# Element-wise work of an attention and two-MLP kernel moved off GpSimd, and the second MLP's weights converted earlier

## The chip, the cores and the metric

One core of one Trainium2 chip runs the kernel. The metric is device time in microseconds (us) of one execution. Before the change three runs took 1559.98, 1563.68 and 1566.03 us; their median is 1563.68.

## What is computed

Float64 inputs are given as they are. For each of 8 batches and 8 heads, 32 packed queries `p` attend to 576 keys and values, and the 576 queries `q` then attend to the packed result. The heads are laid side by side as 4608 tokens of 512 numbers, which pass through two MLPs with hidden width 2048.

```python
p_packed = sm_attn(p, k, v)
out = sm_attn(q, p_packed, p_packed)
x = out.transpose(0, 2, 1, 3).reshape(B * S, H * D)
h = x @ w_in                       # first MLP
x = (h * (1.0 / (1.0 + np.exp(-h)))) @ w_out
h = x @ w_in2                      # second MLP
x = (h * np.cos(h)) @ w_out2
```

## The kernel before

The engines are TensorE (PE), VectorE (DVE), ScalarE (ACT), GpSimd (POOL) and SyncE (SP), whose queue issues every DMA. Precision beyond one pass of the matrix unit comes from splitting a float32 number into a rounded part and a remainder: `split` (L541) makes the first with `copy` (ScalarE or VectorE) and the second with `combine` (a subtraction), and products then take two or three matmuls.

The work runs in two large parts. **The first part** (about the first 812 us) handles the batches in four pairs. `firsts` and `seconds` (L1149, L1154) do a batch's two attentions, `products` (L853) multiplies the packed result into the first MLP's input weights, and `first` (L895) does one step of the first MLP: 6 matmuls into a bank `hb`, a tanh on ScalarE into `gf`, `gf<-gf,hb` on VectorE, `split` into `g`, and 12 matmuls into the four banks `acc`. There are 256 steps, 64 to a pair; a step is counted here by its `gf<-gf,hb`. The `g` ring holds 3 tiles, `hb` 2 banks. Results leave through two `ysb` tiles to DRAM (`ydram`, `ypart`). The first pair's beginning, with its own buffers `ba`, `bat` and its weights' conversion, is called the boot here.

**The second part** does the second MLP in 9 blocks of 8 steps, with a scheme of seven products instead of eight. `load_y` (L970) loads a block (`raw`), forms sums and differences with `combine`, and splits them into `y` (or into freed weight tiles `w`). For its first block that falls into the last steps of the first part, after `change(top, ...)` at L1221 has given the attention's memory to the new tiles.

The weights come as float64 words. `decode` (L556) turns 128x512 of them into float32: two ScalarE and three VectorE instructions on the tiles `wd` and `wy`. For the second MLP, `win2_unit` and `wout2_unit` (L591, L588) decode, combine and split them and write them to DRAM (`w2s`, `w2dram`). They share two `wd` and three `wy` tiles.

**The order** is not written by hand. Every call is recorded as an operation with a price (`price`, L158), the operations that it waits for, and a due time worked out backwards. `schedule` (L297) goes forward in the planner's own time and gives each free engine the ready operation that is due first; `order` (L377) repeats this 8 times and keeps the best. Each engine then runs its list strictly in order. An operation recorded under `either` (L216) may go to whichever of two engines fits better. `release` is the planner's time before which an operation is not ready; `LATER` (L442) is that of the second MLP's weight conversion (set at L1199). The planner's pairs are due to begin at the values of `DUE` (L440), in ns. When POOL is at work, the planner lengthens a VectorE operation on SBUF by half of the overlap (L353).

```python
                if e == self.DVE and o.sbuf and not reverse and free[self.POOL] > t:
                    end += (free[self.POOL] - t) * self.SHARED
...
        if not more:
            plan.release = LATER
```

Of the kernel before, what the change touches and what calls it, by code (L numbers as in the profile page):

```python
# [405 lines left out]
def attention_mlps_kernel(  # L406
# [31 lines left out]
    plan = Plan(nc)  # L438

    DUE = [36e3, 208e3, 380e3, 552e3, 718e3]  # L440

    LATER = 380e3  # L442
    V, A, T, G, DMA = plan.V, plan.A, plan.T, plan.G, plan.D


# [85 lines left out]
            V.tensor_copy(dst, src)  # L531

    def combine(dst, x, y, op):
        if plan.inorder is not None:
            V.tensor_tensor(dst, x, y, op)
            return
        with plan.either():
            V.tensor_tensor(dst, x, y, op)
            G.tensor_tensor(dst, x, y, op)

    def split(d, x):  # L541

        copy(d[:, 0], x)
        combine(d[:, 1], x, f32(d[:, 0]), ALU.subtract)
# [46 lines left out]
    def win2_unit(F, c):  # L591

        def block(y, i, j):
            f = (FH * i + 4 * F) * P
            decode(w_in2[(c + 2 * j) * P : (c + 2 * j + 1) * P, 2 * f : 2 * (f + 4 * P)], y)

        def put(y, prod):
            flat = rings["wd"]().rearrange("p f t -> p (f t)")
            d = flat.bitcast(F32R).rearrange("p (q t f) -> p t q f", q=4, t=2)
            split(d, y.bitcast(F32).rearrange("p (q f) -> p q f", q=4))  # L600
            DMA.dma_start(w2s[F, prod, :, :, c].rearrange("p q t f -> p q (t f)"), flat.bitcast(F32).rearrange("p (q x) -> p q x", q=4))

        y = [rings["wy"]() for _ in range(3)]
        v = [x.bitcast(F32) for x in y]
        block(y[0], 1, 0)
        block(y[1], 1, 1)
        combine(v[2], v[0], v[1], ALU.add)
        put(y[1], 6)
        block(y[1], 0, 0)
        put(y[1], 0)  # L610
        put(y[2], 1)
        combine(v[2], v[2], v[1], ALU.subtract)
        combine(v[0], v[1], v[0], ALU.subtract)
        put(y[2], 2)
        put(y[0], 4)
        block(y[1], 0, 1)
        put(y[1], 3)
        combine(v[1], v[1], v[2], ALU.subtract)
        put(y[1], 5)
# [572 lines left out]
    for pr in range(NPAIR):  # L1192
# [5 lines left out]
        if not more:  # L1198
            plan.release = LATER  # L1199
            for F in range(2):  # L1200
# [6 lines left out]
        for o in range(PAIR[pr + 1] - PAIR[pr]):  # L1207
# [7 lines left out]
            x = o - 48  # L1215
# [51 lines left out]
```

## Time and profile before

| | |
|---|---|
| median of three runs | 1563.68 us (1559.98 to 1566.03) |
| the profiled execution | 1561.91 us, its span 1560.1 us |
| PE busy | 1528.3 us, 98% |
| DVE busy | 1147.5 us, 74%, 2285 instructions |
| ACT busy | 775.9 us, 50%, 1651 instructions |
| POOL busy | 158.8 us, 10%, 161 instructions |
| DMA | 287.30 MB, 184 GB/s over the span |
| mean granted clock of TensorE | 0.992 of full |

The span runs from the first to the last instruction. "Busy" is the time in which at least one instruction of the engine is recorded as running; an instruction's record can overlap the next one's. PE's idle time is what an engine or a DMA makes it wait, beyond the matmuls' own pace.

### The profile page before, as it was taken

What the parts mean: (1) busy time and instruction counts of PE and PEld (TensorE: products, weight loads), DVE (VectorE), ACT (ScalarE), POOL (GpSimd) and SP (SyncE); (2) the same over time, 40 slices, a digit from 0 to 9 for tenths busy, and PEclk for the clock granted to TensorE, in tenths of its full rate; (3) what the DMA queues carried; (4) which work ended last, traced back from release to release, by engine and by line L of the source; (5) the groups of instructions that cost most, each with busy time, mean ns of one, the idle gap of its engine ahead of it and who ended that gap; (6) DMA issues with size and microseconds to landing.
All of it is one profiled execution on the core that took longest, in us unless ns stands there. A gap on an engine that the chain in (4) does not pass through costs nothing.

```text
span 1560.1 us, 31304 instructions
## 1 busy us (share of the span) xinstructions
PE 1528.3 (98%) x11640; PEld 1376.7 (88%) x11640; DVE 1147.5 (74%) x2285; ACT 775.9 (50%) x1651; POOL 158.8 (10%) x161
## 2 busy tenths in 40 slices
PE   9889999999999999999999999999999999999998
PEld 7678978999879898899999999999999999999997
DVE  4997567464688769787657777888887777777665
ACT  5875544334544555555444444444544444444443
POOL 0231001010232204131200000000000000000000
PEclk9899999999999999999999999999999999999999
DMA  9667365221775677556677657878675757575561
GB/s 261 201 217 197 97 140 149 70 40 39 158 210 176 159 191 195 176 169 207 224 240 247 210 191 225 248 220 258 206 238 180 229 176 228 176 221 186 179 199 35
DMA packets 304856, 287.30 MB, mean 184 GB/s; under 512 B 166464, under 2 KB 215104, under 8 KB 304704
## 3 DMA queue, kind: packets, MB, share of 16 engines
q1 hardware_dynamic: 304704, 285.30, 61.5%
q8 instruction: 92, 1.51, 0.4%
q14 instruction: 60, 0.49, 0.1%
HBM read 232.00 MB, written 53.22 MB: 183 GB/s over the span
## 4 chain that ended last, share of the span: by engine, by line
PE 85%; DVE 8%; DMA 3%; ACT 2%; issue 1%; SPq 0%; POOL 0%; DVEq 0%; ACTq 0%; POOLq 0%
PE acc L208 46%; PE hb L208 20%; PE sb L208 10%; PE mb L208 10%; DVE wy L208 1%; DVE wd L208 1%; DMA wd<-in_moe_w_in 1%; DVE big L208 1%; DVE gf L208 1%; DMA ypart<-ysb 1%; DVE w L208 1%; DMA kin<-in_q 0%; DVE rsb L208 0%; DVE g L208 0%; ACT wd L208 0%
## 5 line engine op out<-in xcount | busy, mean ns | idle before, releaser
L208 PE MATMUL acc<-g,w 128*128 128x288 f32 x3072 | 474.0, 298 | 4.8 <-ACT ysb L208 2.7
L208 PEld LDWEIGHTS acc<-g,w 128*128 128x128 f32 x3072 | 426.8, 188 | 34.2 <-issue 21.1
L208 PE MATMUL acc<-w,g 128*128 128x512 f32 x1728 | 431.6, 392 | 0.0
L208 PEld LDWEIGHTS acc<-w,g 128*128 128x128 f32 x1728 | 310.9, 189 | 55.7
L208 PE MATMUL hb<-a,w 128*128 128x288 f32 x1536 | 266.6, 301 | 10.3 <-DVE gf L208 5.7
L208 PEld LDWEIGHTS hb<-a,w 128*128 128x128 f32 x1536 | 223.8, 190 | 29.5 <-issue 11.0
L208 DVE SCALAR_TENSOR_TENSOR gf<-gf,hb 128x288 f32<-128x288 f32 x256 | 112.6, 448 | 72.4 <-ACT gf L208 71.0
L208 ACT ACTIVATE gf<-hb 128x288 f32<-128x288 f32 x256 | 103.4, 410 | 113.3 <-PE hb L208 91.2
L208 POOL TENSOR_TENSOR g<-gf,g 128x288 fp32r<-128x288 f32 x109 | 100.2, 920 | 527.6 <-PE acc L208 276.9
L208 ACT CAST g<-gf 128x288 fp32r<-128x288 f32 x222 | 95.5, 433 | 110.8 <-PE acc L208 69.6
L208 ACT ACTIVATE r<-r,half_pi 128x512 f32<-128x512 f32 x144 | 103.7, 721 | 34.5 <-DVE r L208 34.3
L208 ACT CAST g<-r 128x512 fp32r<-128x512 f32 x144 | 89.5, 621 | 58.6 <-DVE r L208 56.5
L208 DVE TENSOR_TENSOR g<-gf,g 128x288 fp32r<-128x288 f32 x147 | 72.5, 494 | 58.9 <-PE acc L208 35.8
L208 PEld LDWEIGHTS hb<-w,w 128*128 128x128 f32 x729 | 103.8, 190 | 7.9
L208 PE MATMUL hb<-w,w 128*128 128x256 f32 x729 | 110.0, 282 | 0.0
L208 DVE TENSOR_TENSOR g<-r,g 128x512 fp32r<-128x512 f32 x144 | 99.0, 688 | 11.1 <-ACT g L208 10.7
L208 DVE SCALAR_TENSOR_TENSOR r<-n,r 128x512 f32<-128x512 int32 x144 | 99.1, 688 | 2.2
L208 ACT ACTIVATE n<-hb 128x512 int32<-128x512 f32 x72 | 43.1, 598 | 112.9 <-PE hb L208 108.9
L208 DVE TENSOR_TENSOR hb<-hb,gf 128x256 f32<-128x256 f32 x72 | 31.1, 432 | 69.7 <-PE hb L208 69.5
L208 ACT ACTIVATE n<-mb 128x512 int32<-128x512 f32 x36 | 21.5, 598 | 99.7 <-PE mb L208 99.7
L208 PE MATMUL mb<-w,w 128*128 128x256 f32 x456 | 65.6, 282 | 0.0
L208 PE MATMUL sb<-w,w 128*128 128x256 f32 x444 | 64.1, 282 | 0.0
(217 smaller groups left out, 2067.8 us busy)
## 6 DMA issues: line engine op xcount, KB each, us to landing
w<-w2s SPq DMA_DIRECT2D x504, 256.0 KB, 3.6
w2s<-wd SPq DMA_DIRECT2D x28, 512.0 KB, 3.8
wd<-in_moe_w_in SPq DMA_DIRECT2D x24, 512.0 KB, 5.1
w<-w1dram SPq DMA_DIRECT2D x48, 256.0 KB, 3.2
wd<-in_moe_w_out SPq DMA_DIRECT2D x20, 512.0 KB, 4.6
ydram<-ysb SPq DMA_DIRECT2D x64, 144.0 KB, 2.8
raw<-ydram SPq DMA_DIRECT2D x72, 128.0 KB, 4.0
w2dram<-wd SPq DMA_DIRECT2D x16, 512.0 KB, 2.9
```

What stands on the lines that cost most here:

```text
L208: run = lambda: emit(*[real(x) for x in args], **{k: real(x) for k, x in kw.items()})
```

## The change

`combine` no longer offers its operation to GpSimd: sums and differences all go to VectorE. And the conversion of the second MLP's weights is released at 250 us of the planner's time instead of 380, that is within the second pair (208 to 380) instead of at the third pair's beginning.

```diff
-    LATER = 380e3
+    LATER = 250e3
...
     def combine(dst, x, y, op):
-        if plan.inorder is not None:
-            V.tensor_tensor(dst, x, y, op)
-            return
-        with plan.either():
-            V.tensor_tensor(dst, x, y, op)
-            G.tensor_tensor(dst, x, y, op)
+        V.tensor_tensor(dst, x, y, op)
```

Both edits feed the planner, so that every engine's list changes. The number of rows on VectorE goes from 2283 to 2412, on POOL from 165 to 11, none of which is arithmetic of the program. Three places on VectorE follow; `mb` and `sb` are PSUM banks, `big`, `raw`, `wd` and `wy` SBUF tiles.

**The second attention of batch 4, near the 126th step.** Before:

```order
L208 SCALAR_TENSOR_TENSOR gf_148<-gf_148,hb_92 128x288
L208 TENSOR_SCALAR wy_112<-wy_112 128x512
L208 SCALAR_TENSOR_TENSOR wy_112<-wy_112,wd_109 128x512
L208 TENSOR_TENSOR wy_111<-wy_112,wy_111 128x512
L208 STREAM_TRANSPOSE big_177<-sb 128x288
L208 STREAM_TRANSPOSE big_177<-mb 128x288
L208 SCALAR_TENSOR_TENSOR gf_149<-gf_149,hb_93 128x288
L208 TENSOR_REDUCE mxb_129<-big_177 128x18
L208 TENSOR_TENSOR g_152<-gf_149,g_152 128x288
L208 TENSOR_TENSOR big_177<-big_177,mxb_129 128x576
L208 CAST w_102<-sb 128x512
```

After:

```order
L208 SCALAR_TENSOR_TENSOR gf_148<-gf_148,hb_92 128x288
L208 TENSOR_TENSOR a_136<-big_177,a_136 128x576
L208 TENSOR_TENSOR g_151<-gf_148,g_151 128x288
L208 SCALAR_TENSOR_TENSOR gf_149<-gf_149,hb_93 128x288
L208 STREAM_TRANSPOSE big_177<-sb 128x288
L208 STREAM_TRANSPOSE big_177<-mb 128x288
L208 STREAM_TRANSPOSE big_176<-kin_172 128x576
L208 TENSOR_REDUCE mxb_129<-big_177 128x18
L208 TENSOR_TENSOR g_152<-gf_149,g_152 128x288
L208 TENSOR_TENSOR big_177<-big_177,mxb_129 128x576
L208 SCALAR_TENSOR_TENSOR wd_109<-wd_109 128x512
```

The three conversion rows ahead of the transposes are gone; in their place stand `a` and a `g`, which POOL did before.

**VectorE about the 247th step, nine steps before the first part's end.** Before:

```order
L208 TENSOR_TENSOR y_8521<-raw_8511,y_8521 128x256
L208 TENSOR_TENSOR raw_8510<-raw_8512,raw_8510 128x256
L208 SCALAR_TENSOR_TENSOR gf_148<-gf_148,hb_92 128x288
L208 TENSOR_TENSOR y_8522<-raw_8510,y_8522 128x256
L208 TENSOR_TENSOR raw_8518<-raw_8516,raw_8510 128x256
L208 TENSOR_TENSOR y_8523<-raw_8511,y_8523 128x256
L208 TENSOR_TENSOR g_152<-gf_149,g_152 128x288
L208 TENSOR_TENSOR y_8524<-raw_8518,y_8524 128x256
L208 TENSOR_TENSOR raw_8513<-raw_8517,raw_8513 128x256
L208 TENSOR_TENSOR y_8526<-raw_8514,y_8526 128x256
L208 CAST g_150<-gf_148 128x288
L208 TENSOR_TENSOR y_8527<-raw_8515,y_8527 128x256
```

After:

```order
L208 SCALAR_TENSOR_TENSOR gf_149<-gf_149,hb_93 128x288
L208 TENSOR_TENSOR g_151<-gf_148,g_151 128x288
L208 SCALAR_TENSOR_TENSOR gf_148<-gf_148,hb_92 128x288
L208 TENSOR_TENSOR w_1131<-raw_7996,w_1131 128x256
L208 TENSOR_TENSOR g_152<-gf_149,g_152 128x288
L208 TENSOR_TENSOR w_1132<-raw_7997,w_1132 128x256
L208 SCALAR_TENSOR_TENSOR gf_149<-gf_149,hb_93 128x288
```

The first block's sums and splits now stand between the 222nd and the 227th step, 15 of them in one stretch between the 224th and the 225th `gf`.

**VectorE about the 74th step, in the second pair.** Before:

```order
L208 SCALAR_TENSOR_TENSOR gf_149<-gf_149,hb_93 128x288
L208 CAST w_1860<-sb 128x512
L208 TENSOR_TENSOR w_1858<-mb,w_1858 128x512
L208 TENSOR_TENSOR w_1860<-sb,w_1860 128x512
L208 SCALAR_TENSOR_TENSOR gf_148<-gf_148,hb_92 128x288
```

After:

```order
L208 SCALAR_TENSOR_TENSOR gf_149<-gf_149,hb_93 128x288
L208 CAST w_1864<-sb 128x512
L208 SCALAR_TENSOR_TENSOR wd_109<-wd_109 128x512
L208 TENSOR_TENSOR w_1862<-mb,w_1862 128x512
L208 TENSOR_TENSOR w_1864<-sb,w_1864 128x512
L208 TENSOR_TENSOR g_151<-gf_149,g_151 128x288
L208 TENSOR_SCALAR wy_112<-wy_112 128x512
L208 SCALAR_TENSOR_TENSOR wd_108<-wd_108 128x512
L208 SCALAR_TENSOR_TENSOR gf_148<-gf_148,hb_92 128x288
```

The conversion (`wd`, `wy`) begins here; before, its first row stands at the 121st step. It now ends at the 216th step instead of the 240th.

## Rows read from the trace of the kernel before

**Rows 1.** Stretches: busy us (instructions) of each engine, clock, DMA share, GB/s.

```profile
core 0: us, PE busy (x) PEld busy (x) DVE busy (x) ACT busy (x) POOL busy (x), PEclk, DMA share, GB/s
54.80:113.80 59.00, 52.35 (x485) 42.60 (x486) 57.66 (x106) 47.55 (x101) 18.27 (x17) 0.94 0.59 184
113.80:281.40 167.60, 162.87 (x1448) 143.79 (x1447) 112.48 (x235) 87.46 (x215) 20.78 (x23) 1.00 0.57 145
281.40:386.00 104.60, 104.60 (x864) 98.80 (x864) 55.72 (x119) 41.56 (x99) 9.33 (x10) 1.00 0.18 41
386.00:448.50 62.50, 57.66 (x562) 49.31 (x561) 46.15 (x91) 29.77 (x69) 20.60 (x17) 0.97 0.72 170
448.50:755.10 306.60, 304.05 (x2571) 279.69 (x2569) 238.39 (x457) 169.31 (x383) 72.04 (x70) 1.00 0.62 182
755.10:812.00 56.90, 53.16 (x397) 51.74 (x396) 31.81 (x65) 27.74 (x68) 11.68 (x14) 1.00 0.81 253
812.00:1560.10 748.10, 744.21 (x4647) 672.00 (x4647) 571.01 (x1147) 339.60 (x651) 0.00 (x0) 1.00 0.65 203
92.20:99.00 6.80, 5.02 (x28) 2.98 (x28) 6.80 (x12) 4.39 (x10) 2.01 (x2) 0.50 0.87 239
440.40:443.80 3.40, 3.40 (x15) 3.40 (x16) 3.40 (x7) 1.51 (x4) 1.61 (x2) 0.51 0.60 210
```

**Rows 2.** Waits of PE: for whom, us in total, times, longest.

```profile
PE hb L208 <- DVE gf L208: 5.7, 8, 2.6
...
PE acc L208 <- ACT ysb L208: 2.7, 3, 1.5
...
PE acc L208 <- POOL g L208: 0.9, 2, 0.5
```

**Rows 3.** Timeline, end of the first part: start us, us, engine, operation [idle before].

```profile
768.67 1.91 POOL L208 TENSOR_TENSOR y<-raw,y 128x256 fp32r<-128x256 f32 x2 [0.23 <-ACT y L208]
...
769.02 0.96 DVE L208 TENSOR_TENSOR y<-raw,y 128x256 fp32r<-128x256 f32 x1
...
772.73 0.44 DVE L208 SCALAR_TENSOR_TENSOR gf<-gf,hb 128x288 f32<-128x288 f32 x1
...
773.23 0.54 PE L208 MATMUL hb<-a,w 128*128 128x288 f32 x2 [2.63 <-DVE gf L208]
...
774.19 0.41 DVE L208 TENSOR_TENSOR raw<-raw,raw 128x256 f32<-128x256 f32 x1
```

**Rows 4.** Timeline near the 126th step.

```profile
434.58 1.51 POOL L208 TENSOR_TENSOR wd<-wy,wd 128x512 fp32r<-128x512 f32 x1
434.86 1.84 DVE L208 TENSOR_TENSOR big<-big,mxb 128x576 f32<-128x576 f32 x1
...
437.92 0.65 DVE L208 TENSOR_TENSOR w<-mb,w 128x512 fp32r<-128x512 f32 x1
...
438.50 0.67 DVE L208 TENSOR_TENSOR w<-sb,w 128x512 fp32r<-128x512 f32 x1
...
439.22 0.63 PE L208 MATMUL sb<-w,ppf 64*32 64x512 f32 x4 [1.79 <-DVE w L208]
```

**Rows 5.** Timeline in the boot.

```profile
87.87 1.16 POOL L208 TENSOR_TENSOR ba<-ba,rsb 128x576 f32<-128x576 f32 x1 [2.60 <-ACT a L208]
...
87.92 1.72 DVE L208 TENSOR_TENSOR a<-bat,a 128x576 fp32r<-128x576 f32 x1
...
89.70 0.80 PE L208 MATMUL hb<-a,w 128*128 128x288 f32 x4 [1.25 <-DVE a L208]
...
92.40 0.74 DVE L208 TENSOR_TENSOR a<-bat,a 128x576 fp32r<-128x576 f32 x1
```

**Rows 6.** Groups by form: xcount | busy us, mean ns of one | idle before.

```profile
L208 POOL TENSOR_TENSOR g<-gf,g 128x288 fp32r<-128x288 f32 x109 | 100.2, 920 | 527.6 <-PE acc L208 276.9 <-ACT g L208 138.3 <-DVE g L208 37.9
...
L208 DVE TENSOR_TENSOR g<-gf,g 128x288 fp32r<-128x288 f32 x147 | 72.5, 494 | 58.9 <-PE acc L208 35.8 <-ACT g L208 15.3 <-ACT ysb L208 2.3
...
L208 DVE TENSOR_SCALAR r<-r 128x512 f32<-128x512 f32 x144 | 61.0, 424 | 2.6
...
L208 DVE TENSOR_SCALAR wy<-wy 128x512 f32<-128x512 f32 x48 | 27.1, 564 | 0.6 <-ACT wy L208 0.4
```

## Prediction

> **What bounds the kernel now.** The stretches come first [rows 1]. From 812 us on PE is busy 744.21 of 748.10 us and POOL does nothing: that half can only be made faster by fewer matmuls, and the change takes none away. From 281.4 to 386.0 PE is busy for all of the 104.60 us, although POOL works there too. So what the change can win or lose lies where PE is idle in the first part: 6.65 us between 54.8 and 113.8, 4.73 up to 281.4, 4.84 between 386.0 and 448.5, 2.55 up to 755.1 and 3.74 up to 812.0. Twice the clock falls to its lower level, 1.2 GHz (0.50 and 0.51 of 2.4), right after PE stood still: for 6.8 us with PE busy 5.02, and for 3.4 us with PE busy all the time. At full clock that work would take half, so 2.5 and 1.7 us are lost there. The second reading is who ends PE's waits [rows 2]: mostly VectorE, then the output copies `ysb`, and POOL directly for only 0.9 us.
>
> The third reading is why VectorE is late. At the end of the first part VectorE's 128x256 operation takes 0.96 us while POOL runs and 0.41 us when it doesn't; with several of these ahead of it, the `gf` on which PE waits starts at 772.73, and PE has stood still for 2.63 us [rows 3]. Near the 126th step a subtraction on VectorE begins 0.28 us after one on POOL and takes 1.84 us: POOL's ended at 436.09, VectorE's 0.61 us later. PE's wait of 1.79 us hangs on the `w` behind it [rows 4]. In the boot `a` takes 1.72 us beside POOL's 1.16 us and 0.74 us alone, and PE waits 1.25 us for it [rows 5]. So the two engines take turns, and POOL's help is paid for with VectorE's time. That is seen only in operations that have all their operands in SBUF: a `wy` limit of 512 numbers takes 564 ns on average in the first part, the same operation on `r` 424 ns in the second, without POOL [rows 6].
>
> **The change, part by part.** The sum starts from the profiled execution, 1561.9 us; the median of the runs is 1.8 us above it.
>
> *What moves.* A `g` on POOL takes 920 ns, on VectorE 494 with the collisions in it [rows 6]; so work that comes over takes about half the time, and a collision that goes gives back up to 1 us. VectorE is busy 57.66 of 59.0 us in the boot's stretch, but only 46.15 of 62.5 and 31.81 of 56.9 at the other two places [rows 1], so there the added work has room.
>
> *54.8 to 113.8 us.* POOL's 17 instructions come over [rows 1]: 14 `g` at 0.49 and three 576 wide at 0.74 make 9.1 us. The collisions give back 1.0 us each (1.72 less 0.74 [rows 5]); if nine or more of the 17 hit one, VectorE's list is no longer than before, and the chain of `ba`, `bat`, `a`, on which PE waits, no longer goes through an engine that needs 1.16 us a step. The most to be had is the idle time and the clock, 6.65 and 2.5, together 9.2 us. I take half, -4.5 (between -9.2 and +9.1), because that chain is late for more reasons than POOL.
> How far 9.1 is right depends on whether a VectorE instruction costs its recorded time: `w<-sb` starts 0.58 us after `w<-mb`, which is recorded with 0.65 [rows 4]; with 0.07 off each of the 17 the added work is 7.9 us. The Trainium skill ("VectorE: DVE Perf Modes", section "The DRAIN you can't avoid") says that the next operation does not start until the pipe of the one before has emptied. By that rule the whole recorded 9.1 us would count; the row speaks for 7.9.
>
> *Before 54.8 us* a few more of POOL's steps in the boot's chain become 0.4 us shorter each (1.16 against 0.74 [rows 5]): -0.5 (0 to -1.7).
>
> *113.8 to 281.4 us.* The 4.73 us idle there are mostly waits for `ysb` [rows 2], which the change doesn't touch: 0. POOL's own 0.9 us of PE's waits, spread over this stretch and a later one, go: -0.5 in all (0 to -0.9).
>
> *281.4 to 386.0 us.* Here conversion comes in: 48 VectorE instructions between the 72nd and the 112th step that were not there, at 0.58 us (the spacing of 512 wide [rows 4]) 28 us. VectorE goes from 55.72 to about 84 of 104.6 us, and the DMA share is 0.18 there, so its transfers have room. I cost it at nothing, covered by VectorE's idle time; if it is in the way of a `gf`, up to +4.
>
> *386.0 to 448.5 us.* The order no longer has the three `wy` rows ahead of the transposes, and no POOL to collide with. To be had are 4.84 us idle and 1.7 us of the clock. -4 (0 to -6.5): the 1.79 us with its 0.51 clock and the wait before it go, others stay.
>
> *448.5 to 755.1 us.* Fewer conversions and DMAs here, against POOL's 70 instructions that come over. PE is idle for 2.55 us: 0 (-2.5 to +4).
>
> *755.1 to 812.0 us.* The first block's sums have moved some 22 steps ahead; between the 246th and the 248th `gf` three instructions of the block are left. The 2.63 us [rows 3] go, and some of the rest: -3 (0 to -3.7).
>
> *What is late next.* Every list is new, and each engine keeps to its list, so other waits come up. The clearest is the stretch of 15 sums and splits between the 224th and 225th `gf`: at 0.41 us, recorded [rows 3], some 6 us for which a `gf` stands behind them, and behind their loads. PE has two to three steps in hand. For all new waits +4 (0 to +10).
>
> *The second part* is bound by PE, and there `combine` was on VectorE already: 0.
>
> Sum: -4.5 -0.5 -0.5 -4 -3 +4 = -8.5, so 1553.4 against the profiled execution's own 1561.9, and 1555 as a median.
>
> **The rivals.** A measurement of this kernel can tell about 0.5% from no change, that is 7.8 us: below 1555.9 is faster, above 1571.5 slower.
>
> *Nothing that can be told* (0.35). The waits are of the order's making, and new ones take their place. For it: PE is idle for only about 32 us in all (1560.1 less 1528.3 busy), the boot's chain stays long, and a plan dealt anew has had no tuning. With half of the gains and the same new waits, -12.5/2 + 4 = -2, so 1561; this case spans 1556 to 1571. Against it: three of PE's longest waits stand directly behind a collision, and no collision can be left.
>
> *VectorE becomes the bound of the boot; slower* (0.13). Place: 54.8 to 113.8 us, VectorE busy 57.66 of 59.0. If POOL's collisions there hit operations that had time to spare, nothing comes back, the 9.1 us are added to a list that is already full, and PE, fed by it, is late by as much: 1561.9 + 9.1 + 1.8 = 1573 with the other gains used up by the new waits. It decides at nine collisions of 17. Against it: the pairs of rows 5 and of the averages in rows 6. By the 0.58 us spacing it would be 7.9 us, 1571.6, just at the bound.
> The skill's rule on the pipe, above, would speak for the 1573.
>
> *The change doesn't do what it says* (below 0.02): the order has no arithmetic left on POOL and conversions from the 74th step, so only a planner's list that stalls in some way not seen is left of this.
>
> **How the numbers follow.** The forecast, faster with 1546 to 1556 and 1555 the likeliest, has 0.5: it needs about two thirds of the gains at the boot, at the 126th step and at the first part's end, which lie in places far from each other and share one cause. All gains and no new waits would be 1563.7 less 22 (9.2, 1.7, 0.9, 6.5, 3.7), 1542; I hold that all of them come for unlikely. So faster 0.5, same 0.35, slower 0.15 (0.13 and what is unseen). The range 1546 to 1567 leaves out some 0.05 below, and above it the slower case and the edge of the middle one. The likeliest case's own range is 1546 to 1556.
>
> **What would show each step.** Right: VectorE's `wy` limit falls from 564 to about 424 ns and `g` from 494 towards 460; PE's idle time between 54.8 and 113.8 falls by a third or more and the clock's drop near 92 us goes; no wait of 1.8 us and no 0.51 clock near the 126th step; PE busy without a break over the last ten steps of the first part. Wrong: VectorE still busy all the time in the boot and the first `hb` of the 9th step later than before; gaps of PE between 281 and 386 us, ended by `gf` or `g`, where there were none; a wait at the 225th `gf` behind `raw` loads; or gaps of the same sum ended by `ysb`, which would say that the outputs' DMA was the bound behind VectorE. If the time from 812 us on changes by more than 1 us, I have misread the second part.

## The result, and the profile after

The changed kernel takes 1537.05 us (median of four runs, 1535.96 to 1539.94) against 1564.59 for the kernel before (four runs): a ratio of 0.9832, 95% interval 0.9806 to 0.9857. Run again, further below, it took 1540.94 against 1563.04: 0.9860 (0.9845 to 0.9876). So the change gains 22 to 27 us. The forecast was faster with 1555, range 1546 to 1567: the side is right, the size is not, and the time lies 9 us below the range.

The profiled execution took 1536.31 us, its span is 1534.6. The page of the profile, part 1, after:

```profile
PE 1516.4 (99%) x11640; PEld 1371.0 (89%) x11640; DVE 1154.6 (75%) x2413; ACT 786.0 (51%) x1678; POOL 0.7 (0%) x6
```

PE is busy 11.9 us less than before and idle 13.6 us less (31.8 to 18.2). VectorE, with 128 instructions more, is busy only 7 us more. The groups by form after, to be set beside [rows 6] (xcount | busy us, mean ns | idle before):

```profile
L208 DVE TENSOR_TENSOR g<-gf,g 128x288 fp32r<-128x288 f32 x256 | 114.9, 453 | 73.0 <-PE acc L208 52.1 <-ACT g L208 11.7 <-ACT gf L208 2.6
...
L208 DVE TENSOR_SCALAR wy<-wy 128x512 f32<-128x512 f32 x48 | 19.8, 413 | 0.1
```

Both fall as forecast: `g` from 494 to 453 ns, the `wy` limit from 564 to 413. Worked out over the whole trace (for each VectorE operation that lies beside one of POOL, its duration less the median of the same form without POOL), the collisions had lengthened VectorE by 40.7 us; now by nothing.

The stretches after, at the times of [rows 1], and last the only one at the lower clock (busy us and instructions of each engine, clock, DMA share, GB/s):

```profile
54.80:113.80 59.00, 56.22 (x543) 48.61 (x542) 56.51 (x121) 51.62 (x115) 0.00 (x0) 1.00 0.74 226
...
281.40:386.00 104.60, 104.60 (x888) 99.43 (x888) 80.70 (x180) 56.65 (x133) 0.00 (x0) 1.00 0.56 153
386.00:448.50 62.50, 62.50 (x605) 52.20 (x604) 52.80 (x110) 35.27 (x80) 0.00 (x0) 1.00 0.76 197
448.50:755.10 306.60, 306.60 (x2575) 287.56 (x2574) 222.31 (x483) 163.32 (x382) 0.00 (x0) 1.00 0.54 157
755.10:812.00 56.90, 56.07 (x391) 52.68 (x390) 35.41 (x73) 26.02 (x53) 0.00 (x0) 1.00 0.80 248
```
```profile
42.90:49.70 6.80, 5.99 (x97) 5.19 (x97) 5.91 (x14) 4.43 (x11) 0.00 (x0) 0.50 1.05 301
```

From 281 to 755 us PE has no idle time at all, though VectorE's work between 281 and 386 rose from 55.72 to 80.70 us with the conversion that came in. The falls of the clock near 92 and 440 us are gone from this profile. In the other profile of the same kernel (`e10_changed_again`, 1542.3 us) only the one near 440 is gone; its stretches at the lower clock:

```profile
43.00:49.80 6.80, 5.79 (x98) 5.23 (x97) 5.63 (x13) 4.43 (x11) 0.00 (x0) 0.50 1.05 304
87.40:94.20 6.80, 5.69 (x32) 3.68 (x32) 5.47 (x11) 4.77 (x12) 0.00 (x0) 0.50 0.89 261
223.90:227.30 3.40, 3.14 (x14) 3.13 (x14) 2.93 (x6) 1.22 (x4) 0.00 (x0) 0.50 1.01 276
```

Over whole executions the mean granted clock was 0.994 to 0.999 in the eight runs of the changed kernel, and 0.990 to 0.993 in those of the kernel before that were run beside the experiments.

PE's waits after, beside [rows 2] (for whom, us in total, times, longest):

```profile
PE hb L208 <- DVE a L208: 2.2, 2, 2.0
PE hb L208 <- ACT a L208: 1.8, 3, 0.8
PE acc L208 <- ACT ysb L208: 1.8, 3, 1.2
...
PE sb L208 <- DVE w L208: 1.3, 1, 1.3
PE acc L208 <- ACT g L208: 1.2, 1, 1.2
PE mb L208 <- ACT ppf L208: 0.7, 1, 0.7
PE hb L208 <- DVE gf L208: 0.7, 1, 0.7
```

`hb` waited 5.7 us for `gf` before, 0.7 now. Of the waits above 0.5 us two are new, on `g` (1.2) and `ppf` (0.7), both in the first pair.

**Where the time went.** Stretches at fixed times don't hold the same work in two kernels. The table below goes by work instead: a step's beginning is the start of the first of its six matmuls into `hb`, read from each trace. Its seven stretches add up to the span (us).

| stretch | before | after | less |
|---|---|---|---|
| start to step 0 | 37.7 | 39.3 | -1.6 |
| step 0 to 16 (the boot's main part) | 73.2 | 62.6 | 10.6 |
| 16 to 64 (rest of the first pair) | 144.0 | 141.6 | 2.4 |
| 64 to 160 | 279.9 | 269.9 | 10.0 |
| 160 to 240 | 215.7 | 214.3 | 1.4 |
| 240 to the last `hb` | 39.4 | 35.9 | 3.5 |
| last `hb` to the end | 770.2 | 771.0 | -0.8 |
| span | 1560.1 | 1534.6 | 25.5 |

Two stretches carry 20 of the 25.5 us.

### The profile page after: what moved, and what is told of

It is laid out like the page before. It is cut to its first block, busy times and chain, and to the rows that moved or that the text cites. A ratio compares the mean times of both kernels' runs of the same rounds, so it can differ in the third digit from the quotient of the medians.

```text
span 1534.6 us, 31226 instructions
## 1 busy us (share of the span) xinstructions
PE 1516.4 (99%) x11640; PEld 1371.0 (89%) x11640; DVE 1154.6 (75%) x2413; ACT 786.0 (51%) x1678; POOL 0.7 (0%) x6
## 4 chain that ended last, share of the span: by engine, by line
PE 90%; DMA 4%; DVE 3%; ACT 2%; issue 1%; SPq 0%; ACTq 0%; DVEq 0%
PE acc L208 50%; PE hb L208 22%; PE sb L208 9%; PE mb L208 9%; DMA bx<-in_v 1%; DVE r L208 1%; DMA kin<-in_k 0%; DMA ysb<-ypart 0%; DMA ypart<-ysb 0%; DMA w1dram<-w1e 0%; DMA wd<-in_moe_w_in 0%; ACT bkt L208 0%; SPq L208 0%; DVE w L208 0%; DVE g L208 0%
## 5 line engine op out<-in xcount | busy, mean ns | idle before, releaser
L208 PE MATMUL hb<-a,w 128*128 128x288 f32 x1536 | 262.3, 298 | 4.8 <-DVE a L208 2.2
L208 DVE TENSOR_TENSOR g<-gf,g 128x288 fp32r<-128x288 f32 x256 | 114.9, 453 | 73.0 <-PE acc L208 52.1
L208 ACT CAST g<-gf 128x288 fp32r<-128x288 f32 x238 | 102.9, 435 | 122.4 <-PE acc L208 100.7
L208 DVE TENSOR_SCALAR r<-r 128x512 f32<-128x512 f32 x144 | 60.9, 424 | 2.6
## 6 DMA issues: line engine op xcount, KB each, us to landing
ydram<-ysb SPq DMA_DIRECT2D x64, 144.0 KB, 2.5
```

The costliest lines, as they stand in the source:

```text
L208: run = lambda: emit(*[real(x) for x in args], **{k: real(x) for k, x in kw.items()})
```

## The experiments

Twelve experiments, each beside the kernel before on its own chip. The theories that decide it in the end: **A**, the collisions cost the time by themselves, through the operations that they lengthen; **D**, the lists were dealt by a plan that didn't know of the collisions, and what costs is that wrong plan; **F**, the list of the kernel before was merely an unlucky deal.

### Each edit alone

`e1_vector_only`: the first edit without the second.

```diff
-        with plan.either():
-            V.tensor_tensor(dst, x, y, op)
-            G.tensor_tensor(dst, x, y, op)
+        V.tensor_tensor(dst, x, y, op)
```

> Sums and differences all on VectorE, the conversion still released at 380. Theory A (collisions of the two engines cost the time): most of the 27 us come with this edit alone, 1541 to 1548 us, no wait of PE behind a stretched VectorE operation; what stays is at the first part's end, where the first block's sums still fall on the last steps. Theory B (the spread of VectorE's load costs the time): 1555 to 1570, since VectorE has more work in the third and fourth pair than before.

Measured: 1542.54 us (1538.7 to 1546.3), ratio 0.9871 (0.9850 to 0.9892).

`e2_release_only`: the second edit without the first.

```diff
-    LATER = 380e3
+    LATER = 250e3
```

> GpSimd keeps its sums and differences, the conversion is released at 250. Theory A: 1555 to 1565 us; the waits at the boot stay as before and only the 2.6 us at the first part's end and some near the 126th step go. Theory B: 1538 to 1548.

Measured: 1557.39 us, ratio 0.9962 (0.9948 to 0.9977). Both lie in the ranges that A gave. So most of the gain, some 21 us, comes with the sums on VectorE; the release alone gives 6. Whether these 6 belong to the release is taken up again below.

### Collisions without a new order, and the new order with collisions

`e3_same_lists`: plan and lists stay those of the kernel before, but what the plan put on POOL is issued on VectorE, at its planned place. PE, ScalarE and SyncE keep their lists; no collision is left, but VectorE has all the work.

```diff
     def run(self):
         for i in self.order():
-            for f in self.ops[i].emit:
+            o = self.ops[i]
+            for f in [o.choice[self.DVE][1]] if o.engine == self.POOL and o.choice else o.emit:
                 f()
```

> The plan of the kernel before, its lists and places unchanged, but the 154 operations planned for GpSimd are issued on VectorE at the places they were planned for. Theory A: faster than before although nothing was planned anew, 1543 to 1555 us. Theory C (the gain is that the planner found a better list): 1562 to 1580, since VectorE gets work that its list has no room for.

Measured: 1562.04 us, ratio 0.9989 (0.9976 to 1.0002): no gain, against A's 1543 to 1555.

`e4_idle_sums`: the lists of the changed kernel, and beside them POOL adds `gf` to itself into a tile that nobody reads, 110 times.

```diff
+    scr = gp.tile([P, TA], F32, name="scr")
...
         split(g, t)
+        if s % 7 in (0, 2, 4):
+            plan.ops[-1].emit.append(lambda t=t, n=n: nc.gpsimd.tensor_tensor(scr[:, :n], t, t, ALU.add))
```

> The changed kernel, every engine's list the same, and beside it 110 additions of 128x288 on GpSimd (gf + gf into a tile that nobody reads, in 3 steps of every 7), as many as GpSimd had of g before. Theory A: 8 to 20 us slower than the changed kernel, 1545 to 1557, VectorE's g and wy limit stretched as before. Theory C: within 3 us of the changed kernel.

Measured: 1542.06 us (1541.21 to 1550.31), ratio 0.9886 (0.9856 to 0.9916). Against the changed kernel that is 1 to 5 us more by the two medians and 4 to 8 by the two ratios, with intervals that overlap. VectorE is lengthened by 15.7 us (worked out as above), well under half of the 40.7 before. Its groups by form:

```profile
L208 DVE TENSOR_TENSOR g<-gf,g 128x288 fp32r<-128x288 f32 x256 | 122.6, 482 | 66.0 <-PE acc L208 47.6 <-ACT g L208 9.9 <-ACT gf L208 2.5
...
L917 POOL TENSOR_TENSOR scr<-gf 128x288 f32<-128x288 f32 x110 | 87.6, 797 | 675.4 <-DVE gf L208 655.7 <-DVE rsb L208 15.6 <-DVE rs L208 4.1
```

`g` is back at 482 ns. The 1545 to 1557 us that A expected are not reached, but this run alone doesn't settle A: 1 to 8 us for 15.7 us of collisions could be its price. `e3_same_lists` speaks against A in its plain form, since taking the collisions away, while VectorE takes over the work, gives nothing; `e6_true_plan`, further below, decides. What differs is the order of the lists. The boot shows how. From step 0 to step 16 in the kernel before, in `e3_same_lists` and after (stretches, columns as in [rows 1]):

```profile
37.70:110.90 73.20, 62.60 (x600) 49.17 (x596) 71.12 (x131) 57.15 (x121) 21.32 (x19) 0.86 0.68 207
```
```profile
41.30:114.00 72.70, 64.03 (x600) 51.18 (x596) 68.39 (x150) 57.33 (x120) 0.00 (x0) 0.84 0.64 195
```
```profile
39.30:102.00 62.70, 56.40 (x597) 46.70 (x598) 58.84 (x128) 54.93 (x121) 0.00 (x0) 0.95 0.80 224
```

VectorE is busy for 94 to 97% of this stretch in all three, so the stretch can hardly be shorter than VectorE's list. In `e3_same_lists` it does 150 instructions in 68.39 us, in the kernel before 131 in 71.12: the stretch that went and the work that came over are worth the same. After, only 128 instructions lie there. Counted from the start of the program to step 16, VectorE and POOL together carry out 192 operations in the first two kernels and 174 in the changed one. Net, 17 of the 18 fewer are conversion of the first MLP's weights (tiles `wde`, `wd`, `w1e`, `wy` and `w<-wy`), which has moved behind step 16.

### What the plan knows

The section on the kernel before said that the planner lengthens a VectorE operation on SBUF by half of its overlap with POOL (L353). The code reads so, but the charge is never in force: the test asks whether the name of the tile's space ends in "SBUF", and it is "SB". Setting the share `SHARED` to 0 leaves every list as it is. `e5_charge_on` mends only that.

```diff
-        self.ops[-1].sbuf = all(str(raw(x).space).endswith("SBUF") for x in outs + ins)
+        self.ops[-1].sbuf = all(str(raw(x).space).endswith("SB") for x in outs + ins)
```

> The kernel before with the planner's charge for collisions put in force: its test for operands in SBUF compares the name of the memory with SBUF, the name is SB, so that no operation was ever lengthened. GpSimd still does 170 operations. Theory D (the lists are bad because the plan knew nothing of the collisions): 1540 to 1552 us. Theory P (long operations and collisions on GpSimd cost, whatever the plan knows): 1556 to 1568.

Measured: 1553.4 us, ratio 0.9933 (0.9911 to 0.9955), with 170 operations on POOL. That lies between the two ranges, 1.4 us above D's, and its interval overlaps that of a mere new deal (`e12_due_shift`, below): half of the charge shows no effect beyond that of one.

`e6_true_plan` goes the whole way: the two engines block each other in the plan, in both directions, for the four kinds of operation that the trace shows colliding, and POOL costs 2.3 ns per element instead of 2.1.

```diff
-            return 149 + (1.7 if any(0 in [st for st, _ in x.ap] for x in ins) else 2.1) * n, 0
+            return 149 + (1.7 if any(0 in [st for st, _ in x.ap] for x in ins) else 2.3) * n, 0
...
-        self.ops[-1].sbuf = all(str(raw(x).space).endswith("SBUF") for x in outs + ins)
+        self.ops[-1].sbuf = all(str(raw(x).space).endswith("SB") for x in outs + ins) and f in (
+            "tensor_tensor", "scalar_tensor_tensor", "tensor_copy", "tensor_scalar"
+        )
...
+        shares = False
...
-                    end += (free[self.POOL] - t) * self.SHARED
+                    end += free[self.POOL] - t
+                if e == self.POOL and not reverse and shares and free[self.DVE] > t:
+                    end += free[self.DVE] - t
+                if e == self.DVE:
+                    shares = o.sbuf
```

> As the kernel before, with a plan as close to the traces as it goes: GpSimd's price at the 0.81 us that a g takes alone, and of two operations that collide the later one lengthened by all that is left of the other. GpSimd does 162 operations. Theory D: 1538 to 1550 us, at least as good as the one with the charge of half. Theory P: 1556 to 1568.

Measured: 1543.2 us (1541.53 to 1550.88), ratio 0.9880 (0.9849 to 0.9911). POOL still carries out 162 operations and VectorE is still lengthened by 40.4 us, as before; yet the time is that of `e1_vector_only` (0.9871). So A falls: with VectorE lengthened as much as before the time is 20 us shorter. From step 0 to 16:

```profile
42.70:106.80 64.10, 58.38 (x596) 47.69 (x597) 58.19 (x109) 53.29 (x116) 20.37 (x18) 0.92 0.72 215
```

109 instructions on VectorE and 18 on POOL, 64.10 us; up to step 16 the two engines carry out 171 operations, where it was 192. With the half charge it was 180, and 71.0 us.

### Other releases, and the best of both

`e7_release_200` and `e8_release_300` are the changed kernel with `LATER = 200e3` and `300e3`.

> The changed kernel with the conversion released at 200 instead of 250. If the spread of VectorE's load is what the release is good for, nothing more is to be had: 1535 to 1541 us. If the outputs of the first pair (waits for ysb) are hindered by its DMAs, 1540 to 1550.

> The changed kernel with the conversion released at 300. If the gain of the release grows with the time given to the conversion, between the 250 and the 380 of the earlier run: 1537 to 1543 us.

Measured: 1539.06 us, ratio 0.9841 (0.9816 to 0.9865), and 1541.83, 0.9868 (0.9843 to 0.9893). Both lie in their ranges, but the intervals overlap, so no order among the releases is shown.

`e9_true_plan_250` is `e6_true_plan` with `LATER = 250e3`; `e10_changed_again` is the changed kernel, on the same chip.

> Kernel before with the true price of a shared operation in its plan (as in e6_true_plan) and, beside it, the release in the second batch pair (LATER 250). Theory D (the loss came from lists dealt without knowledge of the collisions): the release adds its own 4 to 6 us to the 20 of e6_true_plan, so 1536 to 1541 us, equal to the changed kernel's 1537 within 3 us, although GpSimd still carries out 156 operations. Theory A (GpSimd's collisions cost by themselves): 1541 to 1546, no nearer to the changed kernel than e4_idle_sums came. A time under 1534 would say that GpSimd's help is worth something once its price is known.

> The changed kernel once more, beside e9_true_plan_250 on the same chip, as its yardstick: 1536 to 1540 us by either theory.

Measured: 1542.74 us, ratio 0.9866 (0.9848 to 0.9884), and 1540.94, 0.9860 (0.9845 to 0.9876). The expectation of D held in that the two kernels are equal within 3 us, and missed in that the release added nothing to `e6_true_plan`. `e10_changed_again` itself lies 0.9 us above its range. The absolute time lies where A put it, 2 us above D's; between 1.8 us of difference and intervals that overlap, this run parts nothing. No version here beats the changed kernel, and POOL's operations (159 in the trace, not 156) buy nothing even when they are planned well.

### Was it only another deal?

Every edit deals every list anew, so some of any gain could be luck. Two kernels change the plan by something that has nothing to do with the collisions.

```diff
-            return 149 + (1.7 if any(0 in [st for st, _ in x.ap] for x in ins) else 2.1) * n, 0
+            return 149 + (1.7 if any(0 in [st for st, _ in x.ap] for x in ins) else 2.3) * n, 0
```

> Kernel before with one number changed in its plan, GpSimd's price of 2.1 ns per element raised to 2.3, as in e6_true_plan, but without the mutual waiting of that kernel. Every list is dealt anew. Theory D (lists dealt without the collisions cost 20 us): the collisions are still unknown to the plan, so 1555 to 1566 us, and VectorE's stretch stays at about 40 us. A rival that this study has not yet excluded, F (the list of the kernel before is merely an unlucky deal, and almost any other is better): 1540 to 1552.

```diff
-    DUE = [36e3, 208e3, 380e3, 552e3, 718e3]
+    DUE = [36e3, 210e3, 382e3, 554e3, 718e3]
```

> Kernel before with the beginnings of the three middle batch pairs due 2 us later in the plan, and nothing else: a redeal that has to do with neither GpSimd's price nor the collisions. Theory D: 1557 to 1570 us. Theory F (an unlucky deal): 1540 to 1552.

Measured: `e11_price_only` 1559.93 us, ratio 0.9968 (0.9954 to 0.9982); `e12_due_shift` 1556.74, 0.9949 (0.9935 to 0.9964), 0.3 us below the bound that D gave. VectorE is lengthened by 38.7 and 38.3 us, so the collisions stay. F falls: neither comes near 1552. And `e11_price_only` lacks of `e6_true_plan` only the mutual waiting: with it the ratio goes from 0.9968 to 0.9880. But both beat the kernel before by 4 to 8 us, as the release alone did. From step 0 to 16 in `e12_due_shift`:

```profile
39.10:111.50 72.40, 60.06 (x600) 47.87 (x596) 71.07 (x131) 57.47 (x122) 21.58 (x19) 0.91 0.67 207
```

The boot is as long as before. What this deal improves lies in the middle. The same seven stretches for all kernels (us):

| kernel | to 0 | 0-16 | 16-64 | 64-160 | 160-240 | 240-last | rest | ratio of the times |
|---|---|---|---|---|---|---|---|---|
| before | 37.7 | 73.2 | 144.0 | 279.9 | 215.7 | 39.4 | 770.2 | 1 |
| e3, lists as before | 41.3 | 72.7 | 142.5 | 279.4 | 217.1 | 37.3 | 770.6 | 0.9989 |
| e2, e11, e12: dealt anew, blind | 37.7-42.1 | 70.3-72.4 | 142.3-146.9 | 274.6-276.3 | 216.1-217.4 | 36.9-39.3 | 769.9-771.5 | 0.9949-0.9968 |
| e5, half charge | 37.7 | 71.0 | 144.4 | 277.5 | 216.9 | 40.6 | 767.3 | 0.9933 |
| e6, e9: true plan | 41.9-42.7 | 62.8-64.2 | 144.5-145.9 | 271.3-273.4 | 213.8-214.5 | 36.7-38.2 | 769.6-773.4 | 0.9866-0.9880 |
| e1, e7, e8, e10, after: no POOL | 39.1-45.0 | 62.6-65.3 | 139.5-142.8 | 269.4-272.3 | 214.3-215.3 | 35.9 | 770.2-771.8 | 0.9832-0.9871 |
| e4, idle sums | 39.4 | 60.6 | 142.7 | 272.1 | 214.9 | 35.8 | 774.0 | 0.9886 |

The boot parts the kernels cleanly: 70 us and more where the plan doesn't know the collisions, or half of them, 61 to 65 where it does or has none to know. Part of a boot's length is how long the clock is down in it (0 to 23.9 us in these profiles), which differs between profiles of one kernel. At the same 13.7 us of lower clock the boot takes 70.3 and 72.4 us in `e11` and `e12`, 65.1, 65.1 and 65.3 in `e1`, `e7` and `e10`: 5 to 7 us are not the clock's. The middle (64 to 160) falls in two steps: some 4 us with the three blind deals, some 4 more without POOL or with a true plan. So of the gain of 22 to 27 us, about 4 to 8 is that the kernel before was a poor deal among its like (ratios of the three blind deals, 0.9949 to 0.9968), and the rest, some 15 to 20 (from their mean of 0.9958 to the changed kernel's 0.9832 and 0.9860), is that the plan and the chip agree. The release's own share of the time can't be told from a new deal: with it alone -6 us, with an unrelated shift of 2 us in the plan -8, without POOL 200, 250, 300 and 380 us all lie between 0.983 and 0.987. Only near the 126th step does it show by itself: steps 114 to 130 (58.5 us before, 51.8 after) take 51.8 to 52.8 us in all six profiles with the release at 250 or 200, POOL at work or not, and 54.6 to 58.5 in the eight others.

## Why the prediction was right on the side and wrong on the size

The two profiled executions differ by 25.5 us, the sum had 8.5. Of the 17 us between, 5.6 lie in the boot, 4.7 in steps 130 to 240, 4 in new waits that hardly came, 2.7 near the 126th step. The side came out right, but mostly not for the reason that I gave, the collisions given back: with the collisions gone and the order kept (`e3_same_lists`) the three places that I named, the boot, steps 114 to 130 and step 240 to the last `hb`, gain 0.5, 0.6 and 2.1 us, where the change gains 10.6, 6.7 and 3.5.

**54.8 to 113.8 us, -4.5: the step that failed most.** Steps 0 to 16 gave 10.6 (7.9 in the profile of `e10_changed_again`), more than the "9.2 together" that I named as the most to be had, and not by the way I named, the collisions given back on the chain of `ba`, `bat`, `a`: with every collision gone and the order kept (`e3_same_lists`) the boot takes 72.7 us. That VectorE bounds the boot was right, and the rival that has it slower rested on the same row. What both missed is that the list itself is not fixed: a plan that sees VectorE's load puts 18 operations fewer ahead of step 16. That the plan does so because of the load is argued; that the order carries the gain is shown by `e3_same_lists` and by `e6_true_plan` beside `e11_price_only`.

The rule of the Trainium skill on the pipe ("VectorE: DVE Perf Modes", "The DRAIN you can't avoid") that spoke for the higher price decided nothing, and I cited half of it: the same section says that a next operation which is not held starts earlier. The trace after agrees with that half, as [rows 4] did: two 512 wide `w` start 0.60 us apart, recorded with 0.68:

```profile
87.57 0.68 DVE L208 TENSOR_TENSOR w<-mb,w 128x512 fp32r<-128x512 f32 x1
88.17 0.68 DVE L208 TENSOR_TENSOR w<-sb,w 128x512 fp32r<-128x512 f32 x1
```

**Before 54.8 us, -0.5.** Step 0 came 1.6 us later, and 1.4 in the other profile of the changed kernel; the reason is not shown. And the reading had a hole: "Twice the clock falls" was true from 54.8 us on only. Between 41.0 and 54.6 us of the kernel before there was a third, longer stretch at 1.2 GHz (it is part of step 0 to 16 in the table):

```profile
41.00:54.60 13.60, 11.51 (x125) 8.38 (x125) 13.06 (x24) 8.62 (x19) 3.94 (x3) 0.50 1.01 318
```

After, 6.8 us at that level are left in the first part, of 23.9 in three stretches. Had PE been busy throughout at half speed, the 17.1 us that went were worth 8.5 us (an estimate), where I had counted 4.2. In the profile of `e10_changed_again` only 6.8 us went, worth 3.4 by the same estimate: the clock's share of the gain changes from one execution to the next.

**113.8 to 281.4 us, 0 and -0.5.** Steps 16 to 64 gave 2.4 us. That is within what other deals give or take there (-2.9 to 4.5), so it is no effect of its own. POOL's 0.9 us of PE's waits went, as forecast.

**281.4 to 386.0 us, 0: right.** The 28 us of conversion found room: VectorE's busy time rose by 25.0, the DMA share from 0.18 to 0.56, PE stayed busy without a break, and steps 64 to 114 take 136.7 us before and 136.8 after.

**386.0 to 448.5 us, -4, and 448.5 to 755.1 us, 0: too little.** The wait of 1.79 us and its clock went. Steps 114 to 130 gave 6.7 us, of which the earlier release of the conversion, one of the two reasons that I gave, is worth about 2 to 3 where the lists are dealt without POOL or with the true plan (51.8 to 52.8 us against 54.6 to 55.0). Steps 130 to 240 gave another 4.7, which I had put at 0. Together that is 11.4 us, where PE's visible idle time of 4.84 and 2.55 us and the clock's 1.7 bounded the gain at 9.1. "Idle" in such a row is no bound. A 288 wide matmul is recorded with 298 ns, but the next usually starts 133 ns after it (the median over these steps in the kernel before), so that a wait begins under the record: at the gaps of steps 64 to 240 the starts lie 9.4 us further apart than usual, of which 7.4 show as idle. Such hidden waits and the low clock stand in PE's busy time, which fell by 11.9 us in all with the same 11640 matmuls.

**755.1 to 812.0 us, -3: right, but not for the reason given.** From step 240 on it gave 3.5 us. I had put that down to the first block's sums moving ahead. In `e1_vector_only` they fall on the very last steps, 251 to 255, and the stretch takes the same 35.9 us; in `e2_release_only` they have moved ahead, and it takes 38.1.

**New waits, +4: wrong.** The 15 sums and splits ahead of the 225th `gf` are there, and nothing waits for them. VectorE's timeline after, and the stretch around it:

```profile
687.68 0.42 DVE L208 TENSOR_TENSOR raw<-raw,raw 128x256 f32<-128x256 f32 x1
688.02 0.42 DVE L208 TENSOR_TENSOR y<-raw,y 128x256 fp32r<-128x256 f32 x1
688.37 0.46 DVE L208 TENSOR_TENSOR g<-gf,g 128x288 fp32r<-128x288 f32 x1
688.74 0.42 DVE L208 TENSOR_TENSOR y<-raw,y 128x256 fp32r<-128x256 f32 x1
689.08 1.09 DVE L208 TENSOR_TENSOR raw<-raw,raw 128x256 f32<-128x256 f32 x3
690.09 0.45 DVE L208 TENSOR_TENSOR g<-gf,g 128x288 fp32r<-128x288 f32 x1
690.46 1.42 DVE L208 TENSOR_TENSOR y<-raw,y 128x256 fp32r<-128x256 f32 x4
691.80 0.42 DVE L208 TENSOR_TENSOR raw<-raw,raw 128x256 f32<-128x256 f32 x1
692.13 0.42 DVE L208 TENSOR_TENSOR y<-raw,y 128x256 fp32r<-128x256 f32 x1
692.47 1.09 DVE L208 TENSOR_TENSOR w<-raw,w 128x256 fp32r<-128x256 f32 x3
693.54 0.45 DVE L208 SCALAR_TENSOR_TENSOR gf<-gf,hb 128x288 f32<-128x288 f32 x1
```
```profile
686.00:698.00 12.00, 12.00 (x94) 12.00 (x93) 11.33 (x32) 9.11 (x26) 0.00 (x0) 1.00 0.73 232
```

VectorE is busy for 11.33 of 12 us and PE for all 12. The waits that did come up, `g` 1.2 and `ppf` 0.7, are 1.9 us, under half of the term. I reasoned that a plan dealt anew brings new waits like the old ones. The runs suggest why not, without showing it wait by wait: the old ones came from lists whose prices were wrong by 40 us of VectorE's time, and with right prices the waits that a plan foresees are the ones that come.

**The second part, 0: right** (0.8 us more).

**The rivals.** "Nothing that can be told" and the slower boot both fell. "All gains and no new waits, 1542; unlikely" was the nearest to what happened, and the time went below even that.

## What to carry to other kernels

Where a planner deals the work, ask of a change not only which operations it makes cheaper, but whether it brings the plan's prices nearer to the chip: a shared resource that the plan doesn't know can cost through the order of the lists and not only through the operations that collide. Check that a correction in the planner is in force (switch it off and see whether a list moves) before trusting that it is accounted for. And keep a control that deals the lists anew for no reason: here that alone moved the time by 4 to 8 us, enough to pass for a gain.

## What the runs showed of the hardware that was not expected

- Not every operation in SBUF collides. In `e6_true_plan` VectorE's `wy` limit, 413 ns without POOL, took 1.38 us when it began 0.32 us after one of POOL's, and ended 0.28 us after it; the next on POOL, as wide as the one of 1.16 us in [rows 5], in turn took 1.61. VectorE's timeline with POOL's:

```profile
85.91 1.42 POOL L208 TENSOR_TENSOR ba<-ba,rsb 128x576 f32<-128x576 f32 x1 [1.37 <-DVE rsb L208]
86.23 1.38 DVE L208 TENSOR_SCALAR wy<-wy 128x512 f32<-128x512 f32 x1
87.28 1.61 POOL L208 TENSOR_TENSOR a<-bat,a 128x576 fp32r<-128x576 f32 x1
87.53 0.76 DVE L208 STREAM_TRANSPOSE bat<-ba 128x576 f32<-128x576 f32 x1
88.22 1.22 DVE L208 SCALAR_TENSOR_TENSOR wy<-wy,wde 128x512 int32<-128x512 int32 x1
```

  The limit is held up, and so is the operation at 88.22, alike in form to ones of 0.68 us without POOL. The transpose between them, from SBUF to SBUF too, keeps its 0.76 us under POOL's operation, so "all their operands in SBUF" in my third reading was too wide. The Trainium skill ("SBUF — State Buffer", section "SBUF: two separate sides") says that GpSimd and those VectorE operations that run in a two-port mode or have two SBUF inputs share a port pair, that whichever comes first locks it for its whole instruction, and that the other is fully blocked. The trace agrees in that some operations are held up and the transpose is not; in which mode each runs, it doesn't show. By that rule the limit would end its own 0.41 us after POOL's 87.33, at 87.74 (an estimate); it ended at 87.61, and why 0.13 us sooner is not shown.
- When step 0 starts goes with the clock. In seven profiles, those of `before`, the changed kernel (twice), `e2`, `e4`, `e5` and `e12`, it starts at 37.7 to 39.4 us, without lower clock ahead of it; in the other seven at 41.3 to 45.0, with 6.8 to 10.2 us of it. In the profile of `e6_true_plan` PE stood still for 1.64 us ahead of 27.45, and the clock went to 0.50 for the stretch that follows, with PE busy. In that of the changed kernel the longest stop there was 0.43 us, and the clock stayed up:

```profile
27.45 1.06 PE L208 MATMUL hb<-ident,bx 96*64 96x96 f32 x9 [1.64 <-issue]
```

```profile
27.30:34.10 6.80, 6.65 (x49) 4.71 (x50) 0.97 (x3) 1.88 (x4) 0.00 (x0) 0.50 0.98 261
```
```profile
27.30:34.10 6.80, 6.80 (x92) 4.47 (x94) 4.08 (x9) 2.70 (x6) 0.00 (x0) 1.00 0.96 251
```

  PE gets through 49 matmuls there, against 92. A stop of 1.00 us ahead of 26.51 in `e10_changed_again` was not followed by such a fall. One profiled execution can lie 5 us and more above its kernel's median (`e6_true_plan`: 1550.88 against 1543.2), which is why the experiments above are judged by the runs' ratios, and by stretches that begin at step 0.
